# A two-dimensional Fourier transform and a two-layer network on one core: the next batch's transform cut into finer pieces, and a written row of letters that sets their order among the network's steps

## The chip, the core and the metric

One core of a Trainium2 chip runs the whole program. The metric is the device time of one execution in microseconds (us). Kernels are compared by their median over several executions. One execution was also taken with the profiler; all rows shown here come from it.

## The reference

```python
X = np.fft.fft(np.fft.fft(x, axis=1), axis=2).real     # x: 8 batches, 3008 x 256, f32
h = X.reshape(24064, 256) @ w_in                       # w_in: 256 x 2048
r = np.maximum(h, 0.0)
out = (s * (r * r) + b) @ w_out                        # w_out: 2048 x 256
```

## The kernel before

**The work of a batch.** The input has eight batches. For each one the kernel folds the input rows by symmetry (`load`), makes the transform along the 3008 axis out of these folds as small matrix products with a table (`transform`, once for the even and once for the odd outputs), and sends the result through the network. The transform along the 256 axis is part of the first layer's weights. The network sees a batch as 3 blocks of 502 columns; within a block it walks over 16 slices of the hidden layer. So a batch has 48 steps, numbered 0 to 47 below. All products that need full precision are done as three products of rounded halves (`wd_h`, `wd_l`, `spec_h`, `spec_l`, `gh`, `gl`).

**A step** has two halves. The first, L (`first_layer`), is 6 matmuls on TensorE into a pair of PSUM banks, the tile `ab` (line 629); then three VectorE instructions that make `h` out of `ab` (631 to 633); then on ScalarE a Relu, a Square and a rounding to `gh` (634, 635, 265); then on GpSimd the rest `gl` (266). The second, S (`second_layer`), is 12 matmuls that add `gh` and `gl` times `w_out` into the four PSUM tiles `po` (line 652). After the 16th S of a block (steps 15, 31 and 47), `finish` scales the four `po` into `o` with four VectorE instructions (line 669) and stores them. The next block's first S writes the same four banks.

**Buffers.** There are two `ab` buffers; they are shared by the first layer and by the transform's matmuls. The four `po` fill the other four banks. The tiles `h`, `gh` and `gl` have three buffers each, the loaded `xt` two.

**The next batch's preparation** is cut into pieces by Python generators; each `next()` records the instructions up to the next `yield`. Per batch there are 8 pieces of `load` (each a transfer of 96 x 1024 words and five VectorE instructions, lines 483 to 487: three that work on `xt`, two that write `cs`), and 9 pieces for each of the two transforms: the leaves of the first half, `lf`, with their rounding `fh` on ScalarE; the rest `fl` on VectorE (547); the first pair of tables (8 matmuls into an `ab`, lines 559 and 560, two VectorE instructions that read `ab`, lines 565 and 566, and two more that combine, 570 and 571); the second pair; then `uv`, a second `lf` and `fh`, a second `fl`, and two more pairs, which end in sums `o` and in `store` (ScalarE and GpSimd, `spec_h` and `spec_l`).

**What sets the order.** The engines run what is recorded in program order: `_in_order` chains all instructions of TensorE, VectorE, ScalarE and GpSimd, engine by engine. The transfers on SyncE's queue are placed by the scheduler. For the first batch the order is a row of letters (`START`). After it a loop records one L per step, then the pieces that three tables put there (`LOAD`, `EVEN`, `ODD`, as step numbers), then the S of three steps earlier (`LAG`).

```python
    while step < NB * NBLK * NJ:
        first()
        for gen in extra.get(step - 1, []):
            next(gen)
        if len(pending) > LAG:
            second()
```

Of the kernel before, what the change touches and what calls it, by code (L numbers as in the profile page):

```python
# [15 lines left out]
P = 128  # L16
NB, S, D, FF = 8, 3008, 256, 2048
# [3 lines left out]
R = 96  # L21
# [14 lines left out]
SPLIT = 754  # L36


LOAD = 9, 11, 13, 15, 17, 20, 21, 23
EVEN = 25, 26, 28, 29, 30, 31, 32, 36, 39  # L40
ODD = 40, 41, 43, 44, 45, 46, 47, 52, 55

COPIES = (0, 0), (0, 2), (0, 4), (1, 0), (1, 2)
LOADS = "xxwfxxxxxxw"
WORDS = (
    ("in", 0, 0), ("in", 0, 1), ("in", 1, 0), ("in", 1, 1), ("out", 0), ("out", 1), ("in", 2, 0), ("out", 2),
    ("in", 2, 1), ("out", 3), ("in", 3, 0), ("out", 4), ("in", 3, 1), ("out", 5), ("out", 6), ("out", 7),
)  # L50
START = (
# [192 lines left out]
def kernel(ctx: ExitStack, tc: tile.TileContext, xq, xn, dft, turn, feat, w_in, w_out, s, b, out):  # L244
    nc = tc.nc
# [50 lines left out]
    def decode(part, raw, aux):  # L296

        low, high = raw[:, :, 0], raw[:, :, 1]
        magnitude, bits = aux[:, 0], aux[:, 1]
        rest, w = magnitude.bitcast(F32), bits.bitcast(F32)  # L300
        nc.scalar.activation(rest, high.bitcast(F32), AF.Abs)

        nc.scalar.activation(low, low.bitcast(mybir.dt.uint32), AF.Copy, scale=2.0 ** -29)
        yield

        nc.vector.tensor_scalar(rest, rest, 2.0 ** -15, None, ALU.max)
        nc.vector.tensor_scalar(bits, magnitude, 3, 0x3FFFFFFF, ALU.logical_shift_left, ALU.bitwise_and)
        nc.vector.scalar_tensor_tensor(bits, high, -(1 << 30), bits, ALU.bitwise_and, ALU.bitwise_or)
        yield

        nc.gpsimd.tensor_add(bits, bits, low)
        if part[0] == "out":
            at = slice(2 * part[1], 2 * part[1] + 2)
            split(wo_h[:, at], wo_l[:, at], w.rearrange("p (j d) -> p j d", j=2), nc.gpsimd)
        else:
            halves[part[1:]] = w, rest
        yield
# [158 lines left out]
    def load(su):  # L476

        cs = fold.tile([P, 2, 8, 2 * P], F32, name="cs")
        folded[su] = cs
        for c in range(8):  # L480
            t = stage.tile([R, 4, D], F32, name="xt")
            nc.sync.dma_start(t, xq[su, :, c])
            add(t[:, 0::2], t[:, 0::2], t[:, 1::2])  # L483
            add(t[:, 1], t[:, 0], t[:, 2])  # L484
            sub(t[:, 3], t[:, 0], t[:, 2])  # L485
            add(cs[:R, :, c, :P], t[:, 1::2, :P], t[:, 1::2, P:])  # L486
            sub(cs[:R, :, c, P:], t[:, 1::2, :P], t[:, 1::2, P:])  # L487
            yield

    def load_first(tiles):  # L490

        cs = folded[0]
        for c in range(9):
            if c < 8:
                t = tiles[c]
                add(t[:, 0::2], t[:, 0::2], t[:, 1::2])
                nc.gpsimd.tensor_add(t[:, 1], t[:, 0], t[:, 2])
            if c > 0:
                t = tiles[c - 1]
                add(cs[:R, 0, c - 1, :P], t[:, 1, :P], t[:, 1, P:])  # L500
                nc.gpsimd.tensor_sub(cs[:R, 0, c - 1, P:], t[:, 1, :P], t[:, 1, P:])
            yield

    def load_second(tiles):

        for c, t in enumerate(tiles):
            v = folded[0][:R, 1, c]
            nc.gpsimd.tensor_sub(t[:, 3], t[:, 0], t[:, 2])
            nc.gpsimd.tensor_add(v[:, :P], t[:, 3, :P], t[:, 3, P:])
            nc.gpsimd.tensor_sub(v[:, P:], t[:, 3, :P], t[:, 3, P:])  # L510
            yield

    def store(su, ph, parts):
# [21 lines left out]
    def transform(su, ph):  # L535
# [14 lines left out]
        def pair(leaf, f):  # L550

            fh, fl = f
            ps = two_banks()[:, :, :4 * NL].rearrange("p k (i h g) -> p k i h g", i=2, h=2)
            for kind in range(2):
                at = slice(kind * P, (kind + 1) * P)
                for i in range(2):
                    tab = dft_sb[:, ph, kind, leaf + i]
                    row = leaf % 4 + i
                    nc.tensor.matmul(ps[:, kind, i], fh[:, row, at], tab, start=True, stop=False)  # L559
                    nc.tensor.matmul(ps[:, kind, i, 1], fl[:, row, at], tab[:, 0], start=False, stop=True)  # L560
            if su == 0:
                yield
            t = small.tile([P, 2, 4 * NL], F32, name="t", tag="tmp")
            l = t[:, :, :2 * NL].rearrange("p k (i g) -> p k i g", i=2)
            (nc.scalar.copy if su == 0 and (ph, leaf) in COPIES else nc.vector.tensor_copy)(l, ps[:, :, :, 1])
            add(l, l, ps[:, :, :, 0])
            return t, l

# [183 lines left out]
    def second():  # L752
# [10 lines left out]
        "b": go_on(), "e": go_on(), "w": fold_weights(),  # L763
        "n": nyquist(0, t_ny, room, room_r), "m": nyquist(1, t_ny, room, room_r),
        "s": transform(0, 0), "u": transform(0, 1), "l": load(1),
    }
    for what in START.split():
        if what == "L":
# [54 lines left out]
```

## Time and profile before

| | us |
|---|---|
| median of 3 runs | 1793.42 (1790.34 to 1795.84) |
| the profiled execution | 1803.08 |
| its span, first to last instruction | 1801.0 |
| TensorE busy (matmuls) | 1702.5, 95% of the span |
| VectorE busy | 1489.3, 83% |
| ScalarE busy | 1291.0, 72% |
| GpSimd busy | 964.9, 54% |

Matmuls are pipelined, so a busy TensorE is not one that runs at its peak rate. The mean granted TensorE clock over the span is 0.978 of full speed. The first batch, with the weights' preparation, takes about 326 us; the batches after it are much alike.

### The profile page before, as it was taken

How to read it: one execution, taken by the hardware profiler on the slowest of the kernel's cores; microseconds unless marked ns; L12 is line 12 of the kernel's file. 1: busy time of each engine (PE TensorE's matmuls, PEld its weight loads, DVE VectorE, ACT ScalarE, POOL GpSimd, SP SyncE). 2: the span in 40 equal slices, each digit the busy share in tenths (PEclk: the TensorE clock that was granted, in tenths of full speed). 3: DMA queues.
4: the chain of work that ended last, by engine and by line, in shares of the span. 5: the costliest groups of instructions: out<-in, count | busy, mean ns of one | idle time of the engine just before them, and what ended most of it. 6: DMA issues, size and time to landing. Idle time of an engine off the chain costs nothing.

```text
span 1801.0 us, 21631 instructions
## 1 busy us (share of the span) xinstructions
PE 1702.5 (95%) x7537; PEld 1398.6 (78%) x7537; DVE 1489.3 (83%) x2127; ACT 1291.0 (72%) x1356; POOL 964.9 (54%) x568
## 2 busy tenths in 40 slices
PE   2688899999999999999999999999999999999999
PEld 2365688887888788887788878887788877888887
DVE  7679988899887998889888998879888898885554
ACT  2466577776777778776777777777687767777776
POOL 6556455554456455464455545565455544655554
PEclk9789999999999999999999999999999999999999
DMA  5321200011000210002000110002000020000000
GB/s 151 86 71 55 78 15 24 29 42 58 29 7 24 72 30 27 30 26 73 14 17 29 42 58 29 7 32 65 27 29 29 18 64 7 24 29 7 24 24 23
DMA packets 26100, 68.57 MB, mean 38 GB/s; under 512 B 5444, under 2 KB 10404, under 8 KB 25896
## 3 DMA queue, kind: packets, MB, share of 16 engines
q1 hardware_dynamic: 25464, 64.84, 11.7%
q0 software_dynamic: 528, 2.36, 0.5%
q8 instruction: 59, 0.97, 0.2%
q14 instruction: 49, 0.40, 0.1%
HBM read 42.46 MB, written 24.73 MB: 37 GB/s over the span
## 4 chain that ended last, share of the span: by engine, by line
PE 71%; DVE 17%; issue 6%; ACT 3%; DMA 2%; POOL 1%; SPq 0%; DVEq 0%; POOLq 0%; ACTq 0%
PE po L652 46%; PE ab L629 22%; DVE h L631 3%; DVE h L632 3%; DVE h L633 2%; PE ab L559 2%; DVE xt L484 1%; DVE cs L487 1%; DVE xt L483 1%; DMA xt<-in_xq 1%; PE ab L560 1%; ACT h L635 1%; ACT h L634 1%; DVE fl L547 1%; DVE xt L485 1%
## 5 line engine op out<-in xcount | busy, mean ns | idle before, releaser
L266 POOL TENSOR_TENSOR gl<-h,gh 128x1004 fp32r<-128x1004 f32 x384 | 839.1, 2185 | 788.9 <-ACT gh L265 573.3
L634 ACT ACTIVATE h<-h 128x1004 f32<-128x1004 f32 x384 | 400.6, 1043 | 389.3 <-DVE h L633 384.9
L652 PE MATMUL po<-gh,wo_h 128*128 128x502 f32 (+1 forms) x1536 | 489.2, 399 | 9.0 <-DVE o L669 9.0
L652 PE MATMUL po<-gl,wo_h 128*128 128x502 f32 (+1 forms) x1536 | 480.5, 394 | 1.9 <-POOL gl L641 1.8
L652 PE MATMUL po<-gh,wo_l 128*128 128x502 f32 (+1 forms) x1536 | 480.5, 395 | 0.0
L631 DVE SCALAR_TENSOR_TENSOR h<-ebc,wny,ab 128x502 f32<-128x502 f32 x384 | 281.1, 732 | 223.6 <-PE ab L629 211.2
L635 ACT ACTIVATE h<-h 128x1004 f32<-128x1004 f32 x384 | 401.1, 1045 | 12.2
L265 ACT CAST gh<-h 128x1004 fp32r<-128x1004 f32 x384 | 397.4, 1035 | 16.6 <-PE po L652 4.5
L652 PEld LDWEIGHTS po<-gh,wo_h 128*128 128x128 f32 x1536 | 289.9, 192 | 71.2 <-issue 11.1
L652 PEld LDWEIGHTS po<-gl,wo_h 128*128 128x128 f32 x1536 | 294.4, 192 | 63.3 <-POOL gl L641 3.2
L652 PEld LDWEIGHTS po<-gh,wo_l 128*128 128x128 f32 x1536 | 293.0, 191 | 62.2
L629 PE MATMUL ab<-spec_h,wd_h 128*128 128x502 f32 x768 | 304.2, 396 | 32.7 <-DVE h L633 21.1
L629 PE MATMUL ab<-spec_h,wd_l 128*128 128x502 f32 x768 | 302.9, 394 | 0.1
L629 PE MATMUL ab<-spec_l,wd_h 128*128 128x502 f32 x768 | 301.8, 393 | 0.0
L633 DVE TENSOR_TENSOR h<-h,ab 128x502 f32<-128x502 f32 x384 | 260.4, 678 | 13.3
L632 DVE TENSOR_TENSOR h<-h,ab 128x502 f32<-128x502 f32 x384 | 260.2, 678 | 13.2
L629 PEld LDWEIGHTS ab<-spec_h,wd_h 128*128 128x128 f32 x768 | 147.6, 192 | 71.1 <-DVE h L633 24.4
L629 PEld LDWEIGHTS ab<-spec_l,wd_h 128*128 128x128 f32 x768 | 147.6, 192 | 29.5
L629 PEld LDWEIGHTS ab<-spec_h,wd_l 128*128 128x128 f32 x768 | 146.2, 190 | 30.7 <-DVE wd_l L266 0.8
L559 PE MATMUL ab<-dft_sb,fh 96*128 96x192 f32 x256 | 66.8, 329 | 40.1 <-DMA dft_sb<-in_dft 19.4
L559 PEld LDWEIGHTS ab<-dft_sb,fh 96*128 96x128 f32 x256 | 53.6, 210 | 45.4 <-issue 33.9
L486 DVE TENSOR_TENSOR cs<-xt 96x256 f32<-96x256 f32 x56 | 75.7, 1352 | 1.9
(87 smaller groups left out, 1068.7 us busy)
## 6 DMA issues: line engine op xcount, KB each, us to landing
xt<-in_xq SPq DMA_DIRECT2D x64, 384.0 KB
out<-o SPq DMA_DIRECT2D x46, 502.0 KB
raw<-in_w_in SPq DMA_DIRECT2D x8, 512.0 KB
raw<-in_w_out SPq DMA_DIRECT2D x8, 512.0 KB
ebc<-e_dram SPq DMA_DIRECT2D x16, 251.0 KB
dft_sb<-in_dft POOLq DMA_DIRECT2D x2, 576.0 KB, 14.0
dft_sb<-in_dft POOLq DMA_DIRECT2D x1, 1152.0 KB, 9.7
ebc<-e_dram SPq DMA_DIRECT2D x8, 126.0 KB
```

Of the source, the lines that this page charges most:

```text
L265: nc.scalar.copy(hi, src)
L266: lo_engine.tensor_sub(lo, src, hi.bitcast(F32))
L483: add(t[:, 0::2], t[:, 0::2], t[:, 1::2])
L486: add(cs[:R, :, c, :P], t[:, 1::2, :P], t[:, 1::2, P:])
L559: nc.tensor.matmul(ps[:, kind, i], fh[:, row, at], tab, start=True, stop=False)
L629: nc.tensor.matmul(ps[:, kind], w[:, kind, fj], m[:, kind], start=i == 0, stop=i == 2)
L631: nc.vector.scalar_tensor_tensor(h[:, 0], ebc, wny[:, j:j + 1], ps[:, 0], op0=ALU.mult, op1=ALU.add)
L632: sub(h[:, 1], h[:, 0], ps[:, 1])
L633: add(h[:, 0], h[:, 0], ps[:, 1])
L634: nc.scalar.activation(h, h, AF.Relu)
L635: nc.scalar.activation(h, h, AF.Square)
L652: nc.tensor.matmul(po[2 * pm + dh][:, :n], l[:, j, dh * P:(dh + 1) * P], r[:, pm, :n], start=start and first, stop=stop and last,)
```

## The change

The transform's pieces and the load's are divided further: a load piece becomes two (three instructions on `xt`, then two that write `cs`), and a pair of tables becomes two (its matmuls; then what VectorE does with their result), now in every batch and not only in the first. That makes 16 pieces of load and 13 of each transform. The tables of step numbers and `LAG` are gone. One row of letters, `BATCH`, gives the order for each batch from the second on: L and S are the two halves of a step, `l` a load piece, `v` a piece of the even transform, `o` one of the odd transform. The row may place two L or two S side by side, so the distance from L to S now varies between 2 and 4 steps. `START` is lengthened over the whole first batch and steps 0 to 8 of the second, in the order that the tables gave; `BATCH` begins at step 9 and runs to step 8 of the batch after. Several new tuples name work that could change its engine; they are empty or equal what was there.

```diff
-LAG = 3
-LOAD = 9, 11, 13, 15, 17, 20, 21, 23
-EVEN = 25, 26, 28, 29, 30, 31, 32, 36, 39
-ODD = 40, 41, 43, 44, 45, 46, 47, 52, 55
+BATCH = (
+    "L l S L L S l S L l l S L l l S l L S l L S L S l L l L S S L S l L l S L l S S L l L l S L v l S L S v S L "
...
+)
...
             sub(t[:, 3], t[:, 0], t[:, 2])
+            yield
             add(cs[:R, :, c, :P], t[:, 1::2, :P], t[:, 1::2, P:])
             sub(cs[:R, :, c, P:], t[:, 1::2, :P], t[:, 1::2, P:])
...
-            if su == 0:
-                yield
+            yield
             t = small.tile([P, 2, 4 * NL], F32, name="t", tag="tmp")
...
-    extra = {}
-    for su in range(NB - 1):
-        at = su * NBLK * NJ
-        pieces = ((EVEN, transform(su + 1, 0)), (ODD, transform(su + 1, 1)))
-        for places, gen in ((LOAD, load(su + 1)),) * (su > 0) + pieces:
-            for v in places:
-                extra.setdefault(at + v, []).append(gen)
+    su = 1
     while step < NB * NBLK * NJ:
-        first()
-        for gen in extra.get(step - 1, []):
-            next(gen)
-        if len(pending) > LAG:
-            second()
+        work = {}
+        if su < NB - 1:
+            work = {"l": load(su + 1), "v": transform(su + 1, 0), "o": transform(su + 1, 1)}
+        for what in BATCH.split():
+            if what == "L" and step < NB * NBLK * NJ:
+                first()
+            elif what == "S" and pending:
+                second()
+            elif what in work:
+                next(work[what])
+        su += 1
```

The first place is VectorE's row at steps 17 and 18 of the third batch, up to the four instructions that finish a block. Here are the rows before: `h` of step 17, a load piece, `h` of step 18, the finish.

```order
L631 SCALAR_TENSOR_TENSOR h<-ebc,wny,ab 128x502
L632 TENSOR_TENSOR h<-h,ab 128x502
L633 TENSOR_TENSOR h<-h,ab 128x502
L483 TENSOR_TENSOR xt<-xt 96x2x256
L484 TENSOR_TENSOR xt<-xt 96x256
L485 TENSOR_TENSOR xt<-xt 96x256
L486 TENSOR_TENSOR cs<-xt 96x2x128
L487 TENSOR_TENSOR cs<-xt 96x2x128
L631 SCALAR_TENSOR_TENSOR h<-ebc,wny,ab 128x502
L632 TENSOR_TENSOR h<-h,ab 128x502
L633 TENSOR_TENSOR h<-h,ab 128x502
L669 TENSOR_SCALAR o<-po,sb_s,bias 128x502 x4
```

And these are the rows at the same place with the change, whose line numbers are higher by 10 to 14.

```order
L493 TENSOR_TENSOR xt<-xt 96x2x256
L494 TENSOR_TENSOR xt<-xt 96x256
L495 TENSOR_TENSOR xt<-xt 96x256
L645 SCALAR_TENSOR_TENSOR h<-ebc,wny,ab 128x502
L646 TENSOR_TENSOR h<-h,ab 128x502
L647 TENSOR_TENSOR h<-h,ab 128x502
L497 TENSOR_TENSOR cs<-xt 96x2x128
L498 TENSOR_TENSOR cs<-xt 96x2x128
L645 SCALAR_TENSOR_TENSOR h<-ebc,wny,ab 128x502
L646 TENSOR_TENSOR h<-h,ab 128x502
L647 TENSOR_TENSOR h<-h,ab 128x502
L683 TENSOR_SCALAR o<-po,sb_s,bias 128x502 x4
```

The three `xt` instructions of the load piece moved ahead of the `h` of step 17, and only the two `cs` instructions still stand between it and the `h` of step 18.

The second place is VectorE's row where the even transform begins, around steps 25 to 27. Before, from the leaves `lf` on (the `h` rows are those of steps 26 and 27):

```order
L348 TENSOR_TENSOR lf<-cs 96x256
L349 TENSOR_TENSOR lf<-cs 96x256
L631 SCALAR_TENSOR_TENSOR h<-ebc,wny,ab 128x502
L632 TENSOR_TENSOR h<-h,ab 128x502
L633 TENSOR_TENSOR h<-h,ab 128x502
L547 TENSOR_TENSOR fl<-cs,fh 96x512
L547 TENSOR_TENSOR fl<-lf,fh 96x512
L631 SCALAR_TENSOR_TENSOR h<-ebc,wny,ab 128x502
L632 TENSOR_TENSOR h<-h,ab 128x502
L633 TENSOR_TENSOR h<-h,ab 128x502
```

With the change the `h` rows are those of steps 25 and 26, and another one, of step 27, follows before the first pair's result is read:

```order
L358 TENSOR_TENSOR lf<-cs 96x256
L359 TENSOR_TENSOR lf<-cs 96x256
L497 TENSOR_TENSOR cs<-xt 96x2x128
L498 TENSOR_TENSOR cs<-xt 96x2x128
L645 SCALAR_TENSOR_TENSOR h<-ebc,wny,ab 128x502
L646 TENSOR_TENSOR h<-h,ab 128x502
L647 TENSOR_TENSOR h<-h,ab 128x502
L561 TENSOR_TENSOR fl<-cs,fh 96x512
L561 TENSOR_TENSOR fl<-lf,fh 96x512
L645 SCALAR_TENSOR_TENSOR h<-ebc,wny,ab 128x502
L646 TENSOR_TENSOR h<-h,ab 128x502
L647 TENSOR_TENSOR h<-h,ab 128x502
```

The leaves and `fl` stand one `h` earlier, and the end of the load stands between the leaves and `fl`. On TensorE the first pair's 8 matmuls stay where they were, between the L of step 28 and the S of step 25.

The third place is VectorE's row at steps 30 and 31, where the second pair has been read into `x`. Before, from the `x` rows on:

```order
L570 TENSOR_TENSOR x<-t 128x8x48
L571 TENSOR_TENSOR x<-t 128x8x48
L631 SCALAR_TENSOR_TENSOR h<-ebc,wny,ab 128x502
L632 TENSOR_TENSOR h<-h,ab 128x502
L633 TENSOR_TENSOR h<-h,ab 128x502
L357 TENSOR_TENSOR uv<-cs 96x512
L358 TENSOR_TENSOR uv<-cs 96x512
L631 SCALAR_TENSOR_TENSOR h<-ebc,wny,ab 128x502
```

With the change:

```order
L584 TENSOR_TENSOR x<-t 128x8x48
L585 TENSOR_TENSOR x<-t 128x8x48
L367 TENSOR_TENSOR uv<-cs 96x512
L368 TENSOR_TENSOR uv<-cs 96x512
L645 SCALAR_TENSOR_TENSOR h<-ebc,wny,ab 128x502
L646 TENSOR_TENSOR h<-h,ab 128x502
L647 TENSOR_TENSOR h<-h,ab 128x502
L370 TENSOR_TENSOR lf<-uv 96x256
L371 TENSOR_TENSOR lf<-uv 96x256
L352 SCALAR_TENSOR_TENSOR lf<-uv,turn_sb 96x256 x2
```

The `uv` rows moved ahead of the `h` of step 30, and the second `lf` ahead of the `h` of step 31. The order around it on TensorE, in letters, was L30 v S27, L31 v S28, L32 v S29; it is now L30 v L31 v S27, L32 S28 S29.

## Rows read from the trace of the kernel before

**Rows 1.** Windows, batches two to five: length; PE, PEld, DVE, ACT, POOL busy; clock, DMA, GB/s.

```profile
326.20:537.90 211.70, 208.05 (x929) 172.35 (x928) 183.01 (x261) 156.57 (x160) 112.36 (x59) 0.98 0.11 34
537.90:744.60 206.70, 204.94 (x929) 170.07 (x929) 181.19 (x261) 156.57 (x160) 112.81 (x59) 1.00 0.11 35
744.60:954.70 210.10, 206.51 (x930) 171.24 (x929) 182.98 (x261) 156.52 (x160) 112.24 (x59) 0.99 0.11 34
954.70:1166.30 211.60, 207.97 (x930) 172.52 (x929) 182.85 (x261) 156.56 (x160) 112.47 (x59) 0.98 0.11 34
```

**Rows 2.** TensorE's timeline, last batch, steps 3 to 5: each L's first matmul.

```profile
1601.78 0.39 PE L629 MATMUL ab<-spec_h,wd_h 128*128 128x502 f32 x1
...
1605.88 0.39 PE L629 MATMUL ab<-spec_h,wd_h 128*128 128x502 f32 x1
...
1610.89 0.39 PE L629 MATMUL ab<-spec_h,wd_h 128*128 128x502 f32 x1
```

**Rows 3.** TensorE's timeline, fifth batch, step 19: L's last matmul, S's first two.

```profile
1035.62 0.39 PE L629 MATMUL ab<-spec_h,wd_l 128*128 128x502 f32 x1
1037.34 0.46 PE L652 MATMUL po<-gh,wo_h 128*128 128x502 f32 x1 [1.33 <-DVE o L669]
1037.95 0.49 PE L652 MATMUL po<-gh,wo_h 128*128 128x502 f32 x1 [0.15 <-DVE o L669]
```

**Rows 4.** TensorE's timeline, fifth batch, step 28: L's last matmul, the pair's first.

```profile
1074.51 0.39 PE L629 MATMUL ab<-spec_h,wd_l 128*128 128x502 f32 x1
1077.03 0.50 PE L559 MATMUL ab<-dft_sb,fh 96*128 96x192 f32 x1 [2.14 <-DVE h L633]
```

**Rows 5.** Windows behind these two waits, columns as in rows 1.

```profile
1035.60:1042.40 6.80, 5.31 (x22) 3.79 (x21) 5.83 (x10) 4.04 (x4) 3.44 (x2) 1.00 0.52 202
1077.00:1083.80 6.80, 6.77 (x20) 5.84 (x21) 5.59 (x7) 5.52 (x6) 3.01 (x2) 0.51 0.00 0
```

**Rows 6.** VectorE's timeline, fifth batch, steps 17 and 18: start, length, instruction.

```profile
1028.12 0.73 DVE L631 SCALAR_TENSOR_TENSOR h<-ebc,wny,ab 128x502 f32<-128x502 f32 x1
...
1030.19 0.68 DVE L483 TENSOR_TENSOR xt<-xt 96x512 f32<-96x512 f32 x1
...
1031.70 2.37 DVE L486 TENSOR_TENSOR cs<-xt 96x256 f32<-96x256 f32 x1
1033.99 0.41 DVE L487 TENSOR_TENSOR cs<-xt 96x256 f32<-96x256 f32 x1
1034.33 0.72 DVE L631 SCALAR_TENSOR_TENSOR h<-ebc,wny,ab 128x502 f32<-128x502 f32 x1
...
1036.39 2.92 DVE L669 TENSOR_SCALAR o<-po,sb_s,bias 128x502 f32<-128x502 f32 x4
```

**Rows 7.** GpSimd's timeline at the same time.

```profile
1031.62 2.17 POOL L266 TENSOR_TENSOR gl<-h,gh 128x1004 fp32r<-128x1004 f32 x1 [3.03 <-ACT gh L265]
```

**Rows 8.** VectorE's timeline, fifth batch: `fl`, then `h` of step 27.

```profile
1071.92 2.29 DVE L547 TENSOR_TENSOR fl<-cs,fh 96x512 fp32r<-96x512 f32 x1 [2.11 <-ACT fh L544]
...
1074.74 0.72 DVE L631 SCALAR_TENSOR_TENSOR h<-ebc,wny,ab 128x502 f32<-128x502 f32 x1
```

**Rows 9.** VectorE's timeline, fifth batch, steps 29 and 30: second pair, `uv`.

```profile
1087.55 0.55 DVE L565 COPY t<-ab 128x384 f32<-128x384 f32 x1
...
1089.20 0.55 DVE L571 TENSOR_TENSOR x<-t 128x384 f32<-128x384 f32 x1
...
1092.56 1.19 DVE L357 TENSOR_TENSOR uv<-cs 96x512 f32<-96x512 f32 x1
1093.68 0.68 DVE L358 TENSOR_TENSOR uv<-cs 96x512 f32<-96x512 f32 x1
```

**Rows 10.** VectorE's timeline, fifth batch, steps 39 and 40: last pair, odd leaves.

```profile
1130.39 0.55 DVE L565 COPY t<-ab 128x384 f32<-128x384 f32 x1
...
1133.44 0.73 DVE L631 SCALAR_TENSOR_TENSOR h<-ebc,wny,ab 128x502 f32<-128x502 f32 x1
...
1135.52 1.57 DVE L342 SCALAR_TENSOR_TENSOR lf<-cs,turn_sb 96x256 f32<-96x256 f32 x2
```

More of the change, by code (lines that the diff above doesn't have):

```diff
@@ L36 @@
 SPLIT = 754
-LOAD = 9, 11, 13, 15, 17, 20, 21, 23
-EVEN = 25, 26, 28, 29, 30, 31, 32, 36, 39
-ODD = 40, 41, 43, 44, 45, 46, 47, 52, 55
-COPIES = (0, 0), (0, 2), (0, 4), (1, 0), (1, 2)
+LOWS_ON_VECTOR = ()
+Y_ON_VECTOR = ()
+X_ON_VECTOR = ()
+FIRST_COPIES_ON_SCALAR = (0, 1, 2, 4, 5)
+COPIES_ON_SCALAR = ()
+SUMS_ON_SCALAR = ()
 LOADS = "xxwfxxxxxxw"
@@ L313, in decode @@
             at = slice(2 * part[1], 2 * part[1] + 2)
-            split(wo_h[:, at], wo_l[:, at], w.rearrange("p (j d) -> p j d", j=2), nc.gpsimd)
+            split(
+                wo_h[:, at], wo_l[:, at], w.rearrange("p (j d) -> p j d", j=2),
+                nc.vector if part[1] in LOWS_ON_VECTOR else nc.gpsimd,
+            )
         else:
@@ L496, in load_first @@
                 add(t[:, 0::2], t[:, 0::2], t[:, 1::2])
-                nc.gpsimd.tensor_add(t[:, 1], t[:, 0], t[:, 2])
+                (nc.vector if c in X_ON_VECTOR else nc.gpsimd).tensor_add(t[:, 1], t[:, 0], t[:, 2])
             if c > 0:
@@ L500, in load_first @@
                 add(cs[:R, 0, c - 1, :P], t[:, 1, :P], t[:, 1, P:])
-                nc.gpsimd.tensor_sub(cs[:R, 0, c - 1, P:], t[:, 1, :P], t[:, 1, P:])
+                (nc.vector if c - 1 in X_ON_VECTOR else nc.gpsimd).tensor_sub(
+                    cs[:R, 0, c - 1, P:], t[:, 1, :P], t[:, 1, P:]
+                )
             yield
@@ L507, in load_second @@
             v = folded[0][:R, 1, c]
-            nc.gpsimd.tensor_sub(t[:, 3], t[:, 0], t[:, 2])
-            nc.gpsimd.tensor_add(v[:, :P], t[:, 3, :P], t[:, 3, P:])
-            nc.gpsimd.tensor_sub(v[:, P:], t[:, 3, :P], t[:, 3, P:])
+            engine = nc.vector if c in Y_ON_VECTOR else nc.gpsimd
+            engine.tensor_sub(t[:, 3], t[:, 0], t[:, 2])
+            engine.tensor_add(v[:, :P], t[:, 3, :P], t[:, 3, P:])
+            engine.tensor_sub(v[:, P:], t[:, 3, :P], t[:, 3, P:])
             yield
@@ L560, in pair @@
                     nc.tensor.matmul(ps[:, kind, i, 1], fl[:, row, at], tab[:, 0], start=False, stop=True)
-            if su == 0:
-                yield
+            yield
             t = small.tile([P, 2, 4 * NL], F32, name="t", tag="tmp")
             l = t[:, :, :2 * NL].rearrange("p k (i g) -> p k i g", i=2)
-            (nc.scalar.copy if su == 0 and (ph, leaf) in COPIES else nc.vector.tensor_copy)(l, ps[:, :, :, 1])
+            on_scalar = 4 * ph + leaf // 2 in (COPIES_ON_SCALAR if su else FIRST_COPIES_ON_SCALAR)
+            (nc.scalar.copy if on_scalar else nc.vector.tensor_copy)(l, ps[:, :, :, 1])
             add(l, l, ps[:, :, :, 0])
@@ L665, in finish @@
                 args = sb_s, bias[:, dh:dh + 1]
-                if last and dh:
+                if 2 * pm + dh in SUMS_ON_SCALAR or last and dh:
                     nc.scalar.activation(o[:, dh], po[2 * pm + dh][:, :NT], AF.Identity, scale=args[0], bias=args[1])
@@ L765 @@
         "s": transform(0, 0), "u": transform(0, 1), "l": load(1),
+        "v": transform(1, 0), "o": transform(1, 1),
     }
```

12 rows, old and new, of tables (BATCH, START) are left out of this document.

## The prediction

> **What bounds the kernel now.** I read the windows of whole batches first, then TensorE's timeline for gaps between matmuls, then VectorE's and GpSimd's timelines ahead of each gap. L and S with a number are the halves of that step of a batch, h its three VectorE instructions.
>
> The batches with preparation for a next one are the second to the seventh. Four are in [rows 1]; the sixth and seventh take 211.60 like the fifth. Their sum is 211.7 + 206.7 + 210.1 + 3 x 211.6 = 1263.3 us. Undisturbed, a step takes 1605.88 - 1601.78 = 4.10 us, and one that holds a pair of tables 5.01 [rows 2]. A batch has 48 steps and 8 pairs, so its floor is 48 x 4.10 + 8 x 0.91 = 204.1 us. Six floors are 1224.6; the six batches lose 38.7 us, 6.4 each. That is all the change can win, since the first batch and nine steps of the second keep their order, and the last prepares nothing.
>
> Where a batch loses it shows in TensorE's timeline, in two places. At step 19 TensorE waits before S16, the first of a new block, for the finish of the old one: 1037.34 - 1035.62 instead of 0.23, then 0.61 instead of 0.23, together 1.9 us [rows 3]. At step 28 the first pair waits for an `ab` buffer, for the h of step 27: 1077.03 - 1074.51 is 2.52 instead of 0.23, a loss of 2.3 [rows 4]. Behind this second wait the granted clock is 0.51, the 1.2 GHz level; behind the first, shorter one it stays at 1.00, 2.4 GHz [rows 5]. The window at 0.51 holds 6.8 us with the pair and one S; at full clock these take 0.91 + 12 x 0.228 = 3.6, so the slow clock costs 3.2. The sum, 1.9 + 2.3 + 3.2 = 7.4, is the excess of a 211.6 batch (7.5). The third batch, at 206.7 with a clock of 1.00, has the first loss and little of the second.
>
> So TensorE is the bound, and VectorE's lateness makes its gaps. VectorE is busy 183 of 211.6 us [rows 1], but unevenly: an h takes 2.07 of a step's 4.10 (1028.12 to 1030.19), a load piece 4.14 (1030.19 to 1034.33) [rows 6]. In that piece one instruction takes 2.37 where its twin takes 0.41. It began at 1031.70, just after GpSimd's `gl` (1031.62, 2.17 long), and ended 0.28 after it [rows 6, 7]. A piece that met no `gl` would take 4.14 - 1.95 = 2.2. The Trainium skill, "SBUF — State Buffer", section "Who interferes with whom", states that a VectorE instruction with two SBUF inputs and a GpSimd instruction that reads SBUF exclude each other, and the second to issue waits for the whole of the first. The trace agrees with it, by the 2.37 against 0.41.
>
> **The change, part by part.** No matmul, VectorE, ScalarE or GpSimd instruction is added or removed; only places change. An L is a third of a step on TensorE, 1.37 us, an S 2.73.
>
> *The finish.* From L17's end to S16 TensorE has two steps, 8.2 us, before and after (L18, S14, S15, L19). VectorE's chain is now h17 2.07, load 4.14, h18 2.06 and two of four finish instructions 1.46: 9.7 [rows 6]. That explains 1.5 of the 1.9; the rest is h17's late start. With the change only two `cs` instructions stand between the h: 0.8 free, 2.8 if one meets a `gl`. The chain is 6.4 to 8.4 us, so the wait ends unless VectorE arrives late. The three `xt` instructions ahead of h17 (1.5 free, 3.5 met) have 4.1 - 2.07 = 2.0 us there. In steps 12 to 15 three whole load pieces now fall where two did: 4 x 2.07 + 3 x 2.2 to 4.14 is 14.9 to 20.7, against TensorE's 16.4. So the wait left is 0 to about 4 us; a `gl` takes 2.17 of each 4.10 [rows 7], so that a start is about as likely free as met, and the middle, 17.8, leaves VectorE 1.4 late, within the chain's play of 0 to 1.8: I take 0.3.
>
> *The first pair.* Now `fl` stands behind h26, VectorE idles 2.11 for `fh`, and `fl` takes until 1074.74, 2.8 us [rows 8]; that delay is the wait. With the change `fl` stands one h earlier, with `cs` and h25 between it and its leaves, so that ScalarE makes `fh` meanwhile. From L25's end to the pair TensorE has S22, S23, L26, L27, S24, L28: 12.3 us. VectorE needs h25, `fl`, h26, h27: 3 x 2.07 + 2.8 = 9.0, which spares 3.3 for lateness from the load, whose last half now stands behind h24. The load's stretch, steps 9 to 24, is 16 x 2.07 + 8 x 4.14 + 2.9 = 69.1 on VectorE against 65.6 on TensorE, so it still ends some 3.5 late: the wait is 0 to 2.3, and I take 0.4. Being short, it should not be followed by the slow clock, as the finish wait of 1.9 is not.
>
> *New waits.* (1) `uv` now precedes h30, and L32 needs h30's buffer. TensorE from L29's end: pair 0.91, S26, L30, L31, S27, 9.1 us. VectorE: h29 2.07, pair 2.2, `uv` 1.8 [rows 9], h30 2.07, 8.1, and 0.2 to start, since an L's last matmul lasts 0.39, 0.16 beyond its slot of 0.23 [rows 4]: 0.8 spare. The pair and `uv` hold four instructions that can meet a `gl`, at 1.95 each: 0 to 3.2, and I take 1.0. (2) The odd leaves now precede h40, and L42 needs its buffer. TensorE from L39's end: 8.2 us (S36, L40, S37, L41). VectorE: h39, last pair 3.05, leaves 1.57 [rows 10], h40: 8.8, and 0.2 to start. The wait is 0 to 2.8; 0.8 by this sum, less if the leaves run free, more if others meet a `gl`; I take 0.8. (3) The odd transform's other pieces stand about half a step earlier, with some four us of play (L(n+2) starts 6.8 after L(n) ends, h needs 2.3): 0 to 2, I take 0.3.
>
> *What costs nothing.* Two L side by side, and a distance of 4, hold ScalarE's rounding back until the third S before it has freed `gh`; ScalarE is busy 157 of 211.6 [rows 1], and the S that needs it comes over two steps later. A distance of 2 (S19, S23, S41) leaves 10.9 us from L's end, against h 2.3, three ScalarE instructions of about 1.0 (157 us over 160 [rows 1]) and `gl` 2.2 [rows 7]: 7.5. On SyncE's queue a load waits for the `cs` half two tiles before. The tightest is the fourth: issued after step 12's pieces, needed about 4.4 us later (h13 and a free piece). Its 0.39 MB take 1.9 us at the 202 GB/s of [rows 5], an estimate, so that it is covered; uncovered it would cost VectorE 1 or 2 us in the stretch above. The last batch's only change is its L and S order, with VectorE free: nothing.
>
> **The sum.** Per batch 0.3 + 0.4 + 1.0 + 0.8 + 0.3 = 2.8 us stay of 6.4; six batches keep 16.8 of 38.7 and win 21.9. The profiled execution, 1803.08 (2.1 around its span of 1801.0), would become 1781.2. It stands 9.7 above the median of the runs, which I take as a constant: 1793.42 - 21.9 = 1771.5.
>
> **The rivals.** *Almost all is won.* The new waits fall into VectorE's free time, since the meetings are a matter of phase: the two waits and the slow clock already account for 7.4 of 7.5 us, so the odd pieces cost nothing now. At 0.5 us left per batch the win is 36: 1758.
>
> *A new wait takes the old one's place.* If at L32 or L42 two instructions meet a `gl`, the wait passes 2.3, and the clock falls as in [rows 5]: 2.3 + 3.2 and 1.0 elsewhere are 6.5, as much as now: 1794. For it speaks that both sums above are within 1 us of TensorE's; against it that lateness at one place leaves TensorE waiting, and so spares the next.
>
> *Slower: more load instructions blocked.* A piece in two halves starts twice, and each start can meet a `gl`; now a piece meets about one. If every half met one, VectorE would get 8 x 1.95 = 15.6 us more per batch in a stretch that already ends 3.5 late, with about 4.5 of play. With half of that, 7.8, the waits are 3.5 + 7.8 - 4.5 = 6.8, a slow clock 3.2 and the later waits 2.1: 12.1 against 6.4, so six batches lose 34: 1828. It decides from about one more meeting per batch, 1.95: waits of 1.0, and with a slow clock and the later waits 6.3. The rule named above speaks for this case, as it makes the number of starts the price. Against it: the halves stand mostly right behind an h, and a `gl` of 2.17 fills only half of a step.
>
> **Chances.** The forecast 0.55, with its own range 1764 to 1782 (1.7 to 4.6 us left per batch); almost all won 0.15; a new wait 0.18; slower 0.12. A third of the new-wait case is still faster by over 0.3%, about what a measurement of this kernel can tell from no change: faster 0.75, same 0.12, slower 0.13. The range 1755 to 1793 leaves out the slower case, the upper part of the new-wait case and a little below.
>
> **What would show it.** Right: batches of about 207 us; no wait before S16 at step 19; the pair of step 28 within 0.7 us of L28's last matmul; clock 1.00 in the windows of all six batches; short gaps before L32 and L42, released by h. VectorE's busy time per batch stays within 3 us of 183. Wrong: a gap over 2 us with a window at 0.5 behind it, wherever it stands; VectorE busy 190 or more per batch with `xt` and `cs` instructions of 2.3 us (the slower case); waits on `gl` or `gh` before an S that follows its L by 2; or `xt` waiting for its transfer.

## The result, and the profile after

The changed kernel takes 1767.41 us (median of 4 runs, 1766.68 to 1768.27); the kernel before took 1792.37 beside it (1790.34 to 1795.84). The ratio is 0.9859, with a 95% interval of 0.9842 to 0.9876: faster by 1.4%, 25.0 us. The forecast was 1771.5. Two executions on record stand far from all others and are left out of ranges and ratios, 2095.91 us of the kernel before and 5868.37 us of the kernel with the transform's places alone.

The page of the changed kernel's profiled execution, which took 1766.68 us: span, busy times by engine, and the granted clock in 40 slices.

```profile
span 1764.9 us, 21607 instructions
...
PE 1682.1 (95%) x7537; PEld 1383.4 (78%) x7537; DVE 1429.9 (81%) x2127; ACT 1287.1 (73%) x1356; POOL 967.9 (55%) x568
...
PEclk9799999999999999999999999999999999999999
```

TensorE is busy 20 us less (1702.5 before) though it does the same matmuls, and VectorE 59 us less (1489.3) though it runs the same instructions. The windows of the second to the seventh batch, which answer to [rows 1], say where:

```profile
324.60:529.90 205.30, 204.58 (x929) 169.92 (x928) 173.85 (x259) 153.44 (x158) 112.05 (x58) 1.00 0.11 35
529.90:734.60 204.70, 204.66 (x930) 170.03 (x929) 172.36 (x261) 156.21 (x161) 112.91 (x58) 1.00 0.11 35
734.60:939.20 204.60, 204.58 (x929) 169.97 (x928) 172.29 (x261) 156.06 (x161) 112.94 (x58) 1.00 0.11 35
939.20:1143.90 204.70, 204.66 (x930) 170.03 (x929) 172.42 (x261) 156.20 (x161) 112.92 (x58) 1.00 0.11 35
1143.90:1348.50 204.60, 204.57 (x930) 169.96 (x929) 172.31 (x261) 156.15 (x161) 112.90 (x58) 1.00 0.12 35
1348.50:1553.30 204.80, 204.76 (x929) 169.82 (x928) 173.78 (x261) 156.05 (x161) 112.45 (x58) 1.00 0.09 31
```

A batch takes 204.6 to 205.3 us against a floor of 204.1, at a clock of 1.00 in all six. Together they take 1228.7; before it was 1263.3. So 34.6 of the 36.1 us between the two spans lie in these batches, and only 4.1 us above six floors are left of 38.7. The largest gap left is one that the forecast does not name: in the second batch TensorE waits before L16, whose first matmul starts 1.11 us behind the one ahead of it, a loss of 0.9.

```profile
392.96 0.50 PE L643 MATMUL ab<-spec_h,wd_h 128*128 128x502 f32 x1 [0.72 <-DVE h L647]
```

At the two places of the old waits, TensorE's timeline in the fifth batch at step 19, from the last matmul of the L to the first two of S16 (to be read beside [rows 3]), and at step 28, from L28's last matmul to the first pair's first (beside [rows 4]), reads:

```profile
1020.17 0.39 PE L643 MATMUL ab<-spec_h,wd_l 128*128 128x502 f32 x1
1020.40 0.38 PE L666 MATMUL po<-gh,wo_h 128*128 128x502 f32 x1
...
1020.82 0.50 PE L666 MATMUL po<-gh,wo_h 128*128 128x502 f32 x1
...
1057.42 0.39 PE L643 MATMUL ab<-spec_h,wd_l 128*128 128x502 f32 x1
1057.66 0.25 PE L573 MATMUL ab<-dft_sb,fh 96*128 96x192 f32 x1
```

At step 19 the starts are 0.23 and 0.42 apart (before 1.72 and 0.61), and the next one stands 0.33 behind; with 0.23 as the undisturbed distance, 0.3 us is lost. At step 28 the distance is 0.24 where it was 2.52. Nothing is waited for there any more.

How VectorE gets there in time, at steps 17 and 18 (beside [rows 6]): `h` of step 17, the two `cs` instructions, `h` of step 18, the finish; below it GpSimd's row at that time.

```profile
1012.45 0.74 DVE L645 SCALAR_TENSOR_TENSOR h<-ebc,wny,ab 128x502 f32<-128x502 f32 x1 [0.29 <-PE ab L643]
...
1014.53 0.41 DVE L497 TENSOR_TENSOR cs<-xt 96x256 f32<-96x256 f32 x1
1014.87 2.40 DVE L498 TENSOR_TENSOR cs<-xt 96x256 f32<-96x256 f32 x1
1017.20 0.72 DVE L645 SCALAR_TENSOR_TENSOR h<-ebc,wny,ab 128x502 f32<-128x502 f32 x1
...
1019.26 2.92 DVE L683 TENSOR_SCALAR o<-po,sb_s,bias 128x502 f32<-128x502 f32 x4
```

```profile
1014.83 2.16 POOL L273 TENSOR_TENSOR gl<-h,gh 128x1004 fp32r<-128x1004 f32 x1 [0.63 <-ACT gh L272]
```

An instruction still meets a `gl` here: GpSimd's started at 1014.83 and took 2.16, and the `cs` instruction that started 0.04 us behind it took 2.40 instead of 0.41. As before, one instruction is blocked; but the three `xt` instructions no longer stand in the chain, and from h17's start to h18's it is 4.75 us where it was 6.21 ([rows 6]). And VectorE was on time: it had idled 0.29 before h17. From h17's start to the end of the second finish instruction it is 1019.26 + 1.46 - 1012.45 = 8.3 us, and 0.2 to 0.3 to start, against TensorE's 8.2 from L17's end: the 0.3.

At the first pair, VectorE's `fl` and the `h` of step 28 (beside [rows 8]):

```profile
1050.23 2.29 DVE L561 TENSOR_TENSOR fl<-cs,fh 96x512 fp32r<-96x512 f32 x1
1052.45 0.68 DVE L561 TENSOR_TENSOR fl<-lf,fh 96x512 fp32r<-96x512 f32 x1
...
1057.92 0.74 DVE L645 SCALAR_TENSOR_TENSOR h<-ebc,wny,ab 128x502 f32<-128x502 f32 x1 [0.65 <-PE ab L643]
```

`fl` is no shorter (2.29 both times), but VectorE no longer idles for `fh` ahead of it (2.11 before), and two steps later it is waiting for TensorE, 0.65 us, instead of the other way round.

The load piece, as means over all 56, from VectorE's groups by form: first line, number, total, mean in ns.

```profile
L493 DVE TENSOR_TENSOR xt<-xt 96x512 f32<-96x512 f32 x56 | 71.8, 1281 | 0.0
L497 DVE TENSOR_TENSOR cs<-xt 96x256 f32<-96x256 f32 x56 | 38.5, 687 | 0.7
L495 DVE TENSOR_TENSOR xt<-xt 96x256 f32<-96x256 f32 x56 | 37.1, 662 | 0.0
L498 DVE TENSOR_TENSOR cs<-xt 96x256 f32<-96x256 f32 x56 | 33.1, 592 | 0.0
L494 DVE TENSOR_TENSOR xt<-xt 96x256 f32<-96x256 f32 x56 | 27.3, 487 | 1.9
```

Their sum is 3.71 us; the same five groups of the kernel before sum to 4.17. The pairs' two combining instructions fell too, from 798 and 661 ns to 520 and 459. Each of these means is a mixture of a short time and one that a `gl` lengthens, so that VectorE's 183 us per batch were partly waiting inside instructions, and some 10 of them are gone.

### The profile page after: what moved, and what is told of

Read it like the earlier page. It is cut to its first block, busy times and chain, and to the rows that moved or that the text cites. A ratio compares the mean times of both kernels' runs of the same rounds, so it can differ in the third digit from the quotient of the medians.

```text
span 1764.9 us, 21607 instructions
## 1 busy us (share of the span) xinstructions
PE 1682.1 (95%) x7537; PEld 1383.4 (78%) x7537; DVE 1429.9 (81%) x2127; ACT 1287.1 (73%) x1356; POOL 967.9 (55%) x568
## 4 chain that ended last, share of the span: by engine, by line
PE 86%; DVE 8%; issue 2%; DMA 2%; POOL 1%; ACT 1%; SPq 0%; POOLq 0%; DVEq 0%; ACTq 0%
PE po L666 56%; PE ab L643 28%; PE ab L573 2%; DMA xt<-in_xq 1%; DVE h L645 1%; PE ab L574 1%; DVE h L646 1%; DVE h L647 1%; DVE xt L493 1%; DMA wny<-wny_dram 1%; DVE xt L494 0%; DVE xt L495 0%; DVE fl L561 0%; DVE cs L497 0%; DVE aux L313 0%
## 5 line engine op out<-in xcount | busy, mean ns | idle before, releaser
L666 PE MATMUL po<-gh,wo_h 128*128 128x502 f32 (+1 forms) x1536 | 483.6, 395 | 0.2
L573 PE MATMUL ab<-dft_sb,fh 96*128 96x192 f32 x256 | 62.8, 315 | 30.7 <-DMA dft_sb<-in_dft 19.5
L683 DVE TENSOR_SCALAR o<-po,sb_s,bias 128x502 f32<-128x502 f32 x94 | 68.8, 795 | 8.7 <-PE po L666 8.7
```

Source lines behind the costliest of these rows:

```text
L666: nc.tensor.matmul(po[2 * pm + dh][:, :n], l[:, j, dh * P:(dh + 1) * P], r[:, pm, :n], start=start and first, stop=stop and last,)
```

## Experiments

The kernel before ran beside each; its median was 1790.59 beside the first four told here, 1798.14 beside the half `gl`, the whole pieces and the even halves, and 1793.87 beside the other three. All kernels but the one with half of `gl` are the changed one with other letters in `BATCH`. "Loss" is the distance of two starts less 0.23.

**The division alone.** The row of letters is rewritten to give the old order exactly, both halves of each piece together.

```diff
-    "L l S L L S l S L l l S L l l S l L S l L S L S l L l L S S L S l L l S L l S S L l L l S L v l S L S v S L "
+    "L l l S L S L l l S L S L l l S L S L l l S L S L S L l l S L l l S L S L l l S L S L v S L v S "
...
```

> The changed kernel's code with a row of letters that records the order of before: pieces divided, but the two halves always side by side. My theory (the order makes the gain, the division alone nothing): time of before, 1790 to 1803 us, waits at steps 19 and 28 in every batch, clock 0.5 behind the second in some or all of them. How many of the six batches have the slow clock should differ between executions, which would explain why the profiled one of before stood 10 us above its median. Rival (the new code does something else too): under 1785.

1794.63 us (10 runs, 1790.27 to 1803.62), ratio 1.0033 with an interval of 1.0011 to 1.0055. In its trace TensorE, VectorE, ScalarE and GpSimd run their instructions in the order of before, and both waits are back. Division as such gives nothing; what follows is a matter of places. This kernel showed something else. Its windows of the fifth batch, of the 6.8 us behind the pair's wait at step 28, and the pair's first matmul:

```profile
952.20:1160.70 208.50, 204.86 (x929) 169.86 (x928) 180.96 (x262) 156.97 (x161) 112.59 (x58) 1.00 0.11 34
```

```profile
1076.90:1083.70 6.80, 6.79 (x38) 5.97 (x39) 4.93 (x9) 6.12 (x6) 3.56 (x3) 1.00 0.01 2
```

```profile
1076.91 0.33 PE L573 MATMUL ab<-dft_sb,fh 96*128 96x192 f32 x1 [2.13 <-DVE h L647]
```

The wait is as long as before ([rows 4]: 2.14, here 2.13), but the clock behind it is 1.00 where [rows 5] has 0.51, and the batch takes 208.5 where it took 211.6. So the slow clock costs 3.1 us, the prediction's 3.2, but it does not follow each such wait: it followed all five waits of 2.5 us in the profiled execution of before and two of the five in this one (in both, the third batch's starts are only 0.7 apart).

**The load's places alone.** Steps 9 to 24 as changed, the old order from step 25.

```diff
-    "... L l L l S L v l S L S v S L "
-    "L S L v S v L v v v S L v L v S L S S ..."
+    "... L l L l S L l S L v S L v S "
+    "L S L v v S L v v S L v S L v S L v S ..."
```

> The changed row for steps 9 to 24 without its transform pieces, that is the load's order and the L and S order there; from step 25 on the order of before. Theory (the two waits have separate causes): the finish wait at step 19 goes (1.6 of 1.9 us), the pair's wait at step 28 stays with its slow clock, so batches of 209.5 to 210, 12 us less than the old order. Rival (VectorE's lateness from the load is what makes both): the pair's wait goes too, batches of 205, the whole gain.

1770.82 us (1769.86 to 1771.81), ratio 0.9887 (0.9864 to 0.9910). Batches take 205.1. The finish waits no more, and of the pair's wait a part is left. TensorE at step 28:

```profile
1060.64 0.39 PE L643 MATMUL ab<-spec_h,wd_l 128*128 128x502 f32 x1
1061.77 0.33 PE L573 MATMUL ab<-dft_sb,fh 96*128 96x192 f32 x1 [0.74 <-DVE h L647]
```

1.13 instead of 2.52, a loss of 0.9, with `fl` where it always stood. So most of the pair's wait, too, was lateness brought along from the load.

**The transform's places alone.** The load as before, the changed row from step 24.

```diff
-    "L l S L L S l S L l l S L l l S l L S l L S L S l L l L S S L S l L l S L l S S L l L l S L v l S L S v S L "
+    "L l l S L S L l l S L S L l l S L S L l l S L S L S L l l S L l l S L S L l l S L v S L S v S L "
```

> The load's order of before up to step 23, then the changed row from step 24 on. Theory: the finish wait of 1.9 us stays, the pair's wait and the slow clock go, so batches of about 206 to 207 and 27 us less than the old order in a batch-by-batch sum. Rival (the later pieces need a VectorE that the load left on time): new waits of over 2 us behind step 28, batches of 209 or more.

1794.58 us (10 runs, nine of them 1792.25 to 1796.42), ratio 1.0009 (0.9990 to 1.0028): no gain, though the first pair's letters are the changed ones. The finish loses its 1.9 as before, step 28 still 0.5 (before L28) and 0.7 (before the pair), and a new wait stands before L32. Of VectorE, `uv` and the next `h`; of GpSimd, the `gl` beside them; of TensorE, L32's first matmul:

```profile
1085.91 0.69 DVE L367 TENSOR_TENSOR uv<-cs 96x512 f32<-96x512 f32 x1
1086.52 2.64 DVE L368 TENSOR_TENSOR uv<-cs 96x512 f32<-96x512 f32 x1
1089.09 0.72 DVE L645 SCALAR_TENSOR_TENSOR h<-ebc,wny,ab 128x502 f32<-128x502 f32 x1
```

```profile
1086.42 2.21 POOL L273 TENSOR_TENSOR gl<-h,gh 128x1004 fp32r<-128x1004 f32 x1 [1.42 <-ACT gh L272]
```

```profile
1091.29 0.49 PE L643 MATMUL ab<-spec_h,wd_h 128*128 128x502 f32 x1 [1.49 <-DVE h L647]
```

`uv` began 0.10 us behind a `gl` and took 2.64; L32 began 1.89 us behind the matmul ahead of it, a loss of 1.7. Batches take 209.4 to 209.6, as the rival had it. My theory that the two waits have separate causes, the load's order and `fl`'s place, falls: with the load as it was, the transform's places win little and lose it again four steps later.

**No two L or two S side by side.** The pieces near their changed places, L and S strictly alternating.

```diff
-    "L l S L L S l S L l l S L l l S l L S l L S L S l L l L S S L S l L l S L l S S L l L l S L v l S L S v S L "
+    "L l S L S L l S L l l S L l l S l L S l L S L S l L l S L S L S l L l S L l S L l S L l S L v l S L S v L S "
...
```

> The pieces of the changed row at their places among the L, but L and S strictly in turn, three steps apart. Theory (the pieces' places make the gain): within 0.3% of the changed kernel, batches of 204.5 to 206. Rival (two L or two S side by side are what gives VectorE the time): waits of 1 us or more come back at steps 14 to 19 or 28 to 33, batches of 207 or more, over 0.7% slower than the changed kernel.

1777.56 us (1776.12 to 1778.94), ratio 0.9925 (0.9901 to 0.9948). Batches take 206.3; TensorE waits before L16 (a distance of 1.39, a loss of 1.2) and at step 43, inside the odd transform's first pair, before its first matmul on `fl` (0.97, 0.7). It is 0.6% slower than the changed kernel, between what the theory and the rival asked for. Against this alternating row, whose pieces keep their places only nearly, the uneven steps are worth about 1.7 us a batch, 10 in all.

**Half of `gl`.** The kernel before, in its own order, with GpSimd's instruction on half as many columns: it takes 1.28 us instead of 2.18, and one half of `gl` is left out of the result.

```diff
-        split(gh[:, :, :NT], gl[:, :, :NT], h, nc.gpsimd)
+        nc.scalar.copy(gh[:, :, :NT], h)
+        nc.gpsimd.tensor_sub(gl[:, 0, :NT], h[:, 0], gh[:, 0, :NT].bitcast(F32))
...
-                        po[2 * pm + dh][:, :n], l[:, j, dh * P:(dh + 1) * P], r[:, pm, :n],
+                        po[2 * pm + dh][:, :n], l[:, j, dh * P:(dh + 1) * P], r[:, 0 if r is gl else pm, :n],
```

> The kernel before, with GpSimd's gl made for the first of the two column halves alone (502 of 1004 per partition) and used for both, so that this part of the result is left out; gl then takes about 1.1 instead of 2.2 us and meets fewer VectorE instructions, for a shorter time. Theory (the load's blocked instructions make VectorE late, and that makes both waits): a load piece falls from 4.2 to about 3 us, the waits at steps 19 and 28 shrink below 0.5 us together, batches of 204.5 to 205.5, 1765 to 1770 us. Rival (VectorE's own work and its order make the lateness, blocked or not): a wait of 1.5 us or more stays at step 19, batches of 206.5 or more.

1759.14 us (1758.72 to 1759.33), ratio 0.9793 (0.9752 to 0.9834). The window of the fifth batch, and of GpSimd's groups the `gl`:

```profile
928.20:1133.60 205.40, 205.17 (x929) 170.21 (x929) 165.69 (x261) 156.64 (x161) 69.30 (x59) 1.00 0.11 35
```

```profile
L643 POOL TENSOR_TENSOR gl<-h,gh 128x502 fp32r<-128x502 f32 x384 | 493.4, 1285 | 1091.7 <-ACT gh L642 629.7 <-DVE h L632 322.1 <-DVE h L633 47.3
```

VectorE's instructions and their order are those of before, yet it is busy 166 us per batch instead of 183, the pair's wait is gone, and the finish loses 0.6 instead of 1.9. The piece between h17 and h18 takes 3.15 us where it took 4.14, with one instruction blocked for 1.39 instead of 2.37. So VectorE's lateness in the old order came from the time it spends blocked by `gl`. A shorter `gl` also frees its `h` buffer sooner, but that is not what helped: in the kernel before VectorE waited for a `gl` to free `h` only once in the six batches, 1.9 us. (Its first 327 us also became 15 us shorter, so that the total isn't that of the six batches alone.)

**Whole pieces in the changed order.** Each load piece whole, at the place of its second half.

```diff
-    "L l S L L S l S L l l S L l l S l L S l L S L S l L l L S S L S l L l S L l S S L l L l S L v l S L S v S L "
+    "L S L L S l l S L l l S L l l S L S l l L S L S L l l L S S L S L l l S L S S L l l L S L v l l S L S v S L "
```

> The changed row with the load's pieces undivided: both halves of a piece stand where its second half stood; all else as in the changed row. Theory (the division keeps VectorE from lateness, since five instructions in a row nearly always meet a gl): the waits come back at steps 15 to 19 with 1 us or more per batch, batches of 206 or more, 1775 or more. Rival (the places and the L and S order do it alone): batches within 0.5 us of the changed kernel's 204.7.

1798.83 us (10 runs, 1796.29 to 1802.29), ratio 1.0010 (0.9990 to 1.0029). Batches take 209.4 to 210.6. In all six the finish wait is 3.37 and the slow clock follows. Without the division the new order wins nothing.

**One piece whole.** Only the piece around step 17 is left undivided, between h17 and h18; the other seven stay as changed.

```diff
-    "L l S L L S l S L l l S L l l S l L S l L S L S l L l L S S L S l L l S L l S S L l L l S L v l S L S v S L "
+    "L l S L L S l S L l l S L l l S L S l l L S L S l L l L S S L S l L l S L l S S L l L l S L v l S L S v S L "
```

> The changed row with a single piece undivided: the three xt instructions ahead of the h of step 17 stand behind it, with their two cs instructions; the other seven pieces stay divided. Theory (what stands between the h of step 17 and the finish sets the wait at step 19: h, five load instructions, h, two finish instructions against 8.2 us of TensorE): a wait of 1.3 to 3.4 us at step 19 in every batch, and a slow clock behind it where it passes 2 us, so batches of 206 to 210, 1775 to 1798 us. Rival (the lateness gathered over all undivided pieces made the loss of the run without division): within 0.6 us of 204.7 per batch, under 1772.

1795.47 us (10 runs, 1794.12 to 1799.02), ratio 1.0009 (0.9990 to 1.0028): this single piece takes back the whole gain. VectorE's timeline of the third batch from h17 to the finish, GpSimd's `gl` beside it, and TensorE's last L matmul and first S matmul:

```profile
605.98 0.74 DVE L645 SCALAR_TENSOR_TENSOR h<-ebc,wny,ab 128x502 f32<-128x502 f32 x1 [1.95 <-PE ab L643]
...
608.06 0.68 DVE L493 TENSOR_TENSOR xt<-xt 96x512 f32<-96x512 f32 x1
608.77 2.27 DVE L494 TENSOR_TENSOR xt<-xt 96x256 f32<-96x256 f32 x1
...
611.75 2.38 DVE L498 TENSOR_TENSOR cs<-xt 96x256 f32<-96x256 f32 x1
614.06 0.72 DVE L645 SCALAR_TENSOR_TENSOR h<-ebc,wny,ab 128x502 f32<-128x502 f32 x1
...
616.12 2.92 DVE L683 TENSOR_SCALAR o<-po,sb_s,bias 128x502 f32<-128x502 f32 x4
```

```profile
608.37 2.40 POOL L273 TENSOR_TENSOR gl<-h,gh 128x1004 fp32r<-128x1004 f32 x1 [0.91 <-ACT gh L272]
611.55 2.30 POOL L273 TENSOR_TENSOR gl<-h,gh 128x1004 fp32r<-128x1004 f32 x1 [0.79 <-ACT gh L272]
```

```profile
613.70 0.39 PE L643 MATMUL ab<-spec_h,wd_l 128*128 128x502 f32 x1
617.07 0.47 PE L666 MATMUL po<-gh,wo_h 128*128 128x502 f32 x1 [2.98 <-DVE o L683]
```

VectorE had idled 1.95 before h17, so nothing was late when it began. The piece takes 614.06 - 608.06 = 6.0 us, with two of its five instructions blocked by two different `gl`; S16 comes 3.37 behind L19's last matmul, a loss of 3.1. The window behind it:

```profile
617.00:620.40 3.40, 3.19 (x8) 2.39 (x9) 3.37 (x5) 2.41 (x3) 0.79 (x1) 0.56 0.52 207
```

The clock there is 0.56. The loss of 3.1, another 0.4 before S16's second matmul and some 1.7 of slow clock are the batch's excess over the floor (209.4 against 204.1). So it goes in the third to the seventh batch (209.4 to 210.4); in the second the first distance is 1.97, no slow clock follows, and the batch takes 207.7.

**Halves spread evenly.** The old order, with 16 load halves, one per step from 9 to 24.

```diff
-    "L l S L L S l S L l l S L l l S l L S l L S L S l L l L S S L S l L l S L l S S L l L l S L v l S L S v S L "
+    "L l S L l S L l S L l S L l S L l S L l S L l S L l S L l S L l S L l S L l S L l S L l S L l S L v S L v S "
...
```

> The order of before, but the load's 16 halves spread evenly, one behind the L of each of steps 9 to 24, L and S in turn. Theory (bunched work behind one h is what makes VectorE late): a half of 1.5 to 3 us fits a step of 4.1 less 2.1 for h more often than a piece does, the finish wait at step 19 falls below 0.7 and the pair's at step 28 below 1.3: batches of 205 to 206.5. Rival (the two L side by side are needed too, as the strictly alternating run, 206.3 a batch, may suggest): batches of 207 or more.

1782.45 us (1781.33 to 1786.06), ratio 0.9931 (0.9905 to 0.9956). Batches take 206.7 without the slow clock and 207.9 with it. The pair's starts are 0.5 apart at most, so its wait is nearly gone, but S16's first two matmuls still start 1.93 behind L19's last and 0.62 apart, with the slow clock behind them in three batches: two halves stand between h17 and the finish. The theory held for the pair and failed at the finish. Even spacing serves the pair, not the finish.

**Only what the two waits need.** The changed row up to step 27, which moves `fl` ahead, the old order from step 28.

```diff
-    "L S L v S v L v v v S L v L v S L S S L S L S L S L v S L S v L S v L v o S L S L L o S S L o o S o o S L o "
-    "S L o L S o L S L S L S L S L S o o L S L S L S L o o S L S"
+    "L S L v v S L v v S L v S L v S L v S L S L S L S L v v S L S L S L v v S L o S L o S L S L o o S L o o S L "
+    "o S L o S L o S L S L S L S L S L o o S L S L S L o o S L S"
```

> The changed row for steps 9 to 27, that is the load's order and the leaves and fl one h earlier; from step 28 on the order of before, pairs undivided and uv behind its h. Theory (of the transform's moves only the early fl is worth something, the 0.9 us that stay at step 28 when the load alone is changed; the later moves only add risk): batches of 204.2 to 204.6, 0 to 3 us less than the changed kernel, no gap at step 42. Rival (the later divided pieces are needed): a gap of 0.5 us or more behind step 28, batches over 205.

1766.39 us (1765.57 to 1767.28), ratio 0.9852 (0.9833 to 0.9871). Beside it the changed kernel was run once more:

> The changed kernel once more, for comparison in the same call: 1766 to 1769 us by both theories, batches of 204.6 to 204.8.

1767.62 us (1767.13 to 1768.31), ratio 0.9859 (0.9840 to 0.9878). So the moves of the transform behind step 28 win nothing. Without them batches take 204.1 to 204.5 (205.2 the first), and the changed kernel's gap of 0.33 inside L42, 0.1 lost, is missing. The 1.2 us between the two medians is 0.07%; the runs of the two touch only at their ends, and I take it as equal or very slightly better.

## Why the prediction came out right, and where it did not

The bottleneck was read rightly: VectorE's lateness at two places, made by instructions that a `gl` blocks. Halving `gl` takes most of the lateness away with the order untouched, and the one whole piece brings the finish wait back with everything else as changed.

- **The finish, 0.3 us forecast, 0.3 measured.** The chain came out at the top of its span, 8.3 of 6.4 to 8.4 us, since a `cs` did meet a `gl`. But VectorE was not 1.4 late at h17, as I had it; it had just been idle (0.29). The two errors balance, and that the number is the measured one is luck.
- **The first pair, 0.4 forecast, 0.0 measured.** The load does still end late: in the fifth batch h24 starts 3.0 us behind L24's end, where I had worked out 3.5. What I gave as the cause, `fl` behind its `fh`, is the lesser part of the old wait. The load's places alone took 1.4 of its 2.3 us; the places of the leaves and `fl`, with the L and S around them, take the other 0.9, and without the load's change they did not end the wait.
- **New waits, 2.1 forecast, 0.1 measured.** This is the term that was mis-sized. I priced a meeting with a `gl` at its full 1.95 us and took about the middle of 0 to 3.2 at L32 (two of the four instructions met, 3.1 by the sum; all four would have been 7.0). In the changed kernel's fourth batch `x` began 0.8 us before the end of a `gl` and took 1.21, 0.66 longer than free, and `uv` started level with the next one and ran free; `h` was done 0.5 us before L32 wanted its buffer. The wait is possible all the same: with the old load ahead of it, `uv` fell 0.1 behind a `gl` and L32 lost 1.7. At L42, where I had 0.8, the chain from h39's start to h40's end took 7.9 us instead of 8.8 (1106.63 to 1114.53 in the fifth batch): the odd leaves were not held up and took 0.87 where [rows 10] has 1.57. Whether a `gl` is met, and for how long, is a matter of phase, which my middle values did not give. The rows of VectorE, of GpSimd and of TensorE's L32 in the changed kernel, to be read beside those of the transform's places alone:

```profile
861.53 1.21 DVE L584 TENSOR_TENSOR x<-t 128x384 f32<-128x384 f32 x1
...
863.25 0.69 DVE L367 TENSOR_TENSOR uv<-cs 96x512 f32<-96x512 f32 x1
863.86 0.68 DVE L368 TENSOR_TENSOR uv<-cs 96x512 f32<-96x512 f32 x1
...
865.93 0.68 DVE L647 TENSOR_TENSOR h<-h,ab 128x502 f32<-128x502 f32 x1
```

```profile
860.15 2.18 POOL L273 TENSOR_TENSOR gl<-h,gh 128x1004 fp32r<-128x1004 f32 x1 [0.92 <-ACT gh L272]
863.86 2.70 POOL L273 TENSOR_TENSOR gl<-h,gh 128x1004 fp32r<-128x1004 f32 x1 [1.52 <-ACT gh L272]
```

```profile
867.08 0.39 PE L643 MATMUL ab<-spec_h,wd_h 128*128 128x502 f32 x1
```

- **What costs nothing.** Two L or S side by side cost nothing, as forecast, and more: against the alternating row they are worth some 10 us, which I had not counted. No S waited for its `gh` or `gl`, and no load piece for its transfer.
- **The profiled execution as a constant.** This step was wrong, and it hid the one above. By batches the profiled executions differ by 34.6 us, not 21.9; that is the rival in which almost all is won, and its 1758 would have been too low. The slow clock explains it. A batch of the old order without it takes 208.5, so the profiled execution of before, at 211.7, 210.1 and three times 211.6, held 3.2 + 1.6 + 3 x 3.1 = 14.1 us of slow clock. Without any it would have taken 1803.08 - 14.1 = 1789.0; the median, 1792.37, stands only 3.4 above that. So the median run holds about one slow stretch, not five, and the 9.7 us that I had between profile and median (10.7 with this median) were the others. The granted clocks on record agree: of the old order's executions the twelve at 0.978 or 0.979 took 1801.7 to 1803.6 us, and the 17 at 0.985 to 0.987 took 1788.4 to 1796.5; the changed kernel's eight stand at 0.985 to 0.988. With no slow clock in the changed kernel the profile stands at the median (1766.68 against 1767.41). By this reckoning 3.4 of the 25.0 us won are the clock and 21.6 the rest, waits above all; in the six batches of the profiled pair it is 14.1 and 20.5. The share of the clock in a median run is worked out from times and mean clocks, not seen in a trace.
- **The sum.** I left 16.8 us of waits where 4.1 stayed, and moved the result by a distance of 9.7 that belonged to the slow clock: 12.7 too little gain against about 10 too much. The number was near the time by luck, because the two errors balance, and not by its terms.
- **VectorE's busy time** was to stay within 3 us of 183 per batch; it fell to 172 to 174. The time lost in meetings is not a fixed amount that order can only shift: the better order lost some 10 us less of it.
- **The slower rival** did not come: VectorE's busy time fell. The chain that it priced, blocked load instructions, a wait and a slow clock behind it, is real, but it came from a piece left whole: two blocked instructions, 3.1 of wait and a slow clock. What decides is not how many halves there are, as I had argued, but how many blocked instructions stand between an `h` and the finish.

Left open: whether the old order is really 0.3% slower with the changed code (the interval just excludes no difference, but 1794.63 lies within the medians that the kernel before had beside the other kernels, 1790.59 to 1798.14), and which executions of it get the slow clock.

## What to carry to other kernels

Where a chain on one engine must end before another engine's next block, count what can stand between its last needed result and that end with every blockable instruction at its blocked time, and keep optional pieces out of it; one undivided piece of five instructions at that place cost as much as the whole reordering won. Before an order is priced, test the suspected cause in the old order by shortening the blocker. And set a profiled execution beside the spread of the times: if its excess comes from a state that only some executions have, such as a slow clock behind a wait, price that state apart and don't carry the distance over as a constant.

## What the runs showed of the hardware

The block between VectorE and GpSimd goes both ways, and less than 0.1 us decides which. `uv` starting 0.10 behind a `gl` took 2.64 us, and a `cs` instruction only 0.04 behind one took 2.40 instead of 0.41; `uv` starting level with a `gl` took 0.68, and the `gl` took 2.70 instead of 2.16. The Trainium skill, "SBUF — State Buffer", section "Who interferes with whom", says that who issues first holds the shared pair for the whole instruction. The rows with a distance agree; where the starts are level the trace does not show who issued first, only that `gl` was the one that took longer. This second price is much the smaller: 0.5 us on an engine with half its time free, against 2.0 on the one that TensorE waits for.

The same wait of 2.5 us before the first pair was followed by a granted clock of 0.51 in one execution and of 1.00 in another, with the same instructions around it; and a finish wait of 1.93, behind which I had expected full clock, was followed by the slow one in three of six batches of the kernel with evenly spread halves; one of 1.97 in the kernel with one whole piece was not, and its five of 3.37 all were. And the times follow: the old order's executions lie between 1787 and 1804 us, those of the changed kernel, whose longest wait is about 1 us, between 1766.7 and 1768.3.
